# Expert 0's second weights: three raw units loaded in steps 26 to 30, and all four splits ahead of the last four first-layer blocks

## The chip, the cores and the metric

One core of one Trainium2 chip runs the kernel; the other cores are idle. The metric is the device time of one launch, in microseconds (us), lower is better. TensorE (PE) does the matrix products, VectorE (DVE) and ScalarE (ACT) read what it left in PSUM and work elementwise, GpSimd (POOL) issues the indirect transfers, and SyncE (SP) issues the plain ones.

## What is computed

Attention over 8 batches of 8 heads (576 positions, 64 features), with a plain 32-wide causal window for half of the heads and a dilated one for the rest, and behind it a mixture of eight experts, where each of the 4608 rows goes to the one expert with the largest gate logit:

```python
logits = x @ w_gate
expert_idx = np.argmax(logits, axis=1)
...
for e in range(E):
    mask = expert_idx == e
    ...
    h = np.maximum(xe @ w1[e], 0.0)      # 512 -> 1024
    ye = h @ w2[e]                       # 1024 -> 512
    out[mask] = gate_w[mask, None] * ye
```

## The kernel before

**Attention** runs as a software pipeline of 36 tiles of 128 positions. `step(n)` holds one stage of each of several tiles: scores of tile n, the transposes and the exponential of n-1, the product with v of n-2, the transposes of the rows for the gate of n-3, logits of n-4. Queries and keys of a tile are loaded five steps ahead (`load_qk`, 576 KB), values three steps ahead (`load_v`, 520 KB), both by SP. Every nine tiles `route` ranks the rows by expert; that of the last nine tiles runs as a tail behind the last step: DVE makes a one-hot tile `s1` and a block tile `b1` for each of nine tiles (L552, L560), PE sums them into `tb` (L571), and seven DVE operations over 128x320 tables (L647, L651 and five recorded under L441) give the row lists `both_i` that the later gathers read.

**Expert 0** starts early, on 256 rows taken from the first half of the sequence. Its weights are eight *units* of 128x1024: units 0 to 3 are the first layer, 4 to 7 the second. A unit is loaded by SP into one of three buffers `raw` (L829) and then *split* into a rounded high part (ACT, L730, two casts of 128x512) and the rest (DVE, L731, two subtractions); a product of the split numbers takes three matrix products. The first layer makes eight blocks of h; block f is twelve products into a PSUM tile `hps` (L846), a relu on ACT (L857) and a subtraction on DVE (L858), after which `hps` is free. Blocks 0 to 3 are made in the attention's last steps. Blocks 4 to 7 come behind `att.close()`, with two PSUM buffers for blocks 4, 6 and 7 (tag A) and one for block 5 (tag D): block 7 needs the buffer of block 4.

`att.close()` gives back the memory of the attention's pools, among them `fix` (qkr, vr, the constants `ca` that L552 reads) and `ap`. The pools opened behind it lie in that memory: `ph` with the h tiles first, then `pw1` with units 4 to 7.

**The second layer** of expert 0 follows in a section ordered by hand: `layer2(0, range(6))`, `layer2(1, range(6))` (18 products each, L877; block f of h with unit 4 + f/2), then the gathered rows of the next blocks are turned (`r0.prep_x`, L913), and the rest of expert 0 and the experts 1 to 7 follow.

**What sets the order.** Inside `manual_schedule` the named engines keep the order of the program. Steps 0 to 34 are such a section, for PE, DVE, ACT and SP; expert 0's second layer is another, for PE, DVE and ACT. What lies outside (step 35 on, the route's tail, blocks 4 to 7 and the splits of units 4 to 7) is put in order when the program is built: each engine's queue is filled with whatever is ready by the builder's own estimate, and among ready instructions the one that stands first in the program goes first. On the chip each queue then runs in that fixed order. Loads of `early_load` for units 4 to 6 stand in steps 36 to 38, outside the first section. `split_unit` is L726 to L734.

Of the kernel before, what the change touches and what calls it, by code (L numbers as in the profile page):

```python
# [159 lines left out]
def attention_moe_kernel(ctx, tc, qk, v, wg, w, cst, tok, end, slots, mask, zero, out):  # L160
# [48 lines left out]
    total = NPR * NT  # L209
# [470 lines left out]
    def all_gates():  # L680

        whole = [scr, none, late_g]
        for tab, to in zip(gtabs, whole):
            nc.scalar.dma_start(to, tab[:].rearrange("(p b) o -> p (b o)", p=P))
        whole = [g.bitcast(I32) for g in whole]
        nc.gpsimd.tensor_tensor(whole[0], whole[0], whole[1], op=ALU.add)
        nc.gpsimd.tensor_tensor(whole[0], whole[0], base.bitcast(I32), op=ALU.add)
        nc.gpsimd.tensor_tensor(both_i[:, :NBK, 1], whole[2], whole[0], op=ALU.add)
        nc.sync.dma_start(list_d[:].rearrange("(p b) o -> p b o", p=P), both_i)
# [33 lines left out]
    def new_unit(grp):  # L723
        return pools["w", grp].tile([P, 2, DF], F32R, tag=f"w{grp}", name="wu")

    def split_unit(grp, raw):  # L726
        u = new_unit(grp)
        for i in range(2):
            sl = slice(i * DM, (i + 1) * DM)
            nc.scalar.copy(u[:, 0, sl], raw[:, sl])  # L730
            nc.vector.tensor_tensor(  # L731
                u[:, 1, sl], raw[:, sl], u[:, 0, sl].bitcast(F32), op=ALU.subtract
            )
        return u  # L734
# [346 lines left out]
    def at(n, f, *a):  # L1081
        todo.setdefault(n, []).append(lambda: f(*a))
# [34 lines left out]
        at(FIRST_W + u, early_load, u)  # L1117
        at(FIRST_W + 2 + u, early_split, u)
    for u in range(4, 7):
        at(total + u - 4, early_load, u)  # L1120

    def early_layer1(f):
        n = first.ns
# [313 lines left out]
    for i in range(NE):  # L1437
        st_ = statics[i]
        nx = statics[i + 1] if i + 1 < NE else None
        if i == 0:  # L1440
            for f in range(4, 8):
                st_.layer1([f])
                raw = early.pop(f) if f in early else st_.load(f)
                st_.units.append(split_unit(1, raw))
            r0, r1 = rest0
            with tc.manual_schedule(engines=ENGS):
                ahead = nx.ahead

                def bring(u):
                    ahead[u] = nx.load(u)  # L1450

                def part(u):
                    nx.units.append(split_unit(c if u < 4 else a, ahead.pop(u)))
                    if u < 5:
                        bring(u + 3)

                def some_gates(n):
                    for _ in range(n):
                        gates_later.pop(0)()

                nx.begin()
                r0.fetch_x()
                nx.fetch(0)
                r1.fetch_x()
                nx.fetch(1)
                for u in range(3):
                    bring(u)
                st_.layer2(0, range(6))
                some_gates(1)
                st_.layer2(1, range(6))  # L1470
                r0.prep_x()
                nx.fetch(2)
                some_gates(1)
                st_.layer2(0, range(6, 8))
                r0.layer1([0])
                some_gates(1)
                nx.prep(0)
                nx.fetch(3)
                part(0)
                some_gates(1)  # L1480
                r0.layer1([1])
                some_gates(1)
                r0.turn([0])
                r1.prep_x()
                r0.turn([1])
                st_.layer2(1, range(6, 8))
                some_gates(1)
                r0.layer2(range(4))
                part(1)
                nx.prep(1)  # L1490
                some_gates(1)
                r1.layer1([0])
                some_gates(1)
                nx.prep(2)
                part(2)
                some_gates(1)
                r1.layer1([1])
                r1.turn([0])
                nx.prep(3)
                r1.turn([1])  # L1500
                part(3)
                r0.layer2(range(4, 8))
                part(4)
                r1.layer2()
                all_gates()
                r0.close()
                r1.close()
            loaded += [(nx, a, u, ahead.pop(u)) for u in range(5, 8)]
            a, b_, c = c, a, b_
            continue  # L1510
        with tc.manual_schedule(engines=ENGS):
            one_place(i)
        a, b_, c = c, a, b_
# [51 lines left out]
```

## Time and profile before

| what | us |
|---|---|
| median of three runs | 627.34 |
| lowest and highest | 626.08, 628.61 |
| the profiled execution, its own time | 627.71 |
| its span in the profile | 625.9 |

The profiled execution has 1.81 us around its span. In a row of the timeline the columns are start, duration, engine, line, operation, output<-inputs, form and count; a bracket gives the time for which the engine stood idle just before it, and who ended that. SPq is SP's queue: the row is the issue of a transfer, not the transfer.

### The profile page before, as it was taken

What the parts mean: (1) busy time and instruction counts of PE and PEld (TensorE: products, weight loads), DVE (VectorE), ACT (ScalarE), POOL (GpSimd) and SP (SyncE); (2) the same over time, 40 slices, a digit from 0 to 9 for tenths busy, and PEclk for the clock granted to TensorE, in tenths of its full rate; (3) what the DMA queues carried; (4) which work ended last, traced back from release to release, by engine and by line L of the source; (5) the groups of instructions that cost most, each with busy time, mean ns of one, the idle gap of its engine ahead of it and who ended that gap; (6) DMA issues with size and microseconds to landing.
All of it is one profiled execution on the core that took longest, in us unless ns stands there. A gap on an engine that the chain in (4) does not pass through costs nothing. (4 is left out here: it accounts for less than half of the span.)

```text
span 625.9 us, 13313 instructions
## 1 busy us (share of the span) xinstructions
PE 601.3 (96%) x5299; PEld 490.4 (78%) x5299; DVE 340.5 (54%) x754; ACT 313.2 (50%) x606; POOL 249.3 (40%) x296
## 2 busy tenths in 40 slices
PE   7999999999989999999999999999999999999992
PEld 6877787788878888788888888888888888888771
DVE  3876787888593544563457255625643573453000
ACT  2668766676533541563456256535644563552110
POOL 0336666476826620451245125312522341253520
PEclk8999999999999999999999999999999999999997
DMA  8999999994237650573476267717743763476710
GB/s 319 411 384 414 413 403 410 396 331 139 66 99 230 208 185 29 181 257 117 151 241 231 84 221 240 241 55 236 259 162 112 243 234 119 172 241 252 276 49 21
DMA packets 43359, 138.17 MB, mean 221 GB/s; under 512 B 9008, under 2 KB 10416, under 8 KB 43248
## 3 DMA queue, kind: packets, MB, share of 16 engines
q1 hardware_dynamic: 23088, 78.30, 34.5%
q0 software_dynamic: 19776, 58.52, 27.0%
q8 instruction: 42, 0.69, 0.4%
q10 hardware_dynamic: 432, 0.49, 0.2%
q14 instruction: 21, 0.17, 0.1%
HBM read 117.65 MB, written 21.63 MB: 223 GB/s over the span
## 5 line engine op out<-in xcount | busy, mean ns | idle before, releaser
L731 DVE TENSOR_TENSOR wu<-raw,wu 128x512 fp32r<-128x512 f32 x200 | 128.7, 687 | 103.7 <-ACT wu L730 103.7
L877 PE MATMUL yps<-wu,h 128*128 128x512 f32 x696 | 170.5, 396 | 0.4 <-DVE wu L731 0.4
L846 PE MATMUL hps<-x,wu 128*128 128x512 f32 (+1 forms) x720 | 164.0, 385 | 0.2 <-DVE h L858 0.2
L846 PEld LDWEIGHTS hps<-x,wu 128*128 128x128 f32 x720 | 132.0, 188 | 27.6 <-DVE h L858 0.7
L877 PEld LDWEIGHTS yps<-wu,h 128*128 128x128 f32 x696 | 128.0, 188 | 27.4 <-DVE wu L731 0.8
L730 ACT CAST wu<-raw 128x512 fp32r<-128x512 f32 x200 | 113.3, 621 | 27.8 <-DMA raw<-in_w_dram,wi 17.2
L922 POOL DMA_INDIRECT raw<-in_w_dram,wi x40 | 39.4, 985 | 98.3 <-DVE wu L731 90.7
L858 DVE SCALAR_TENSOR_TENSOR h<-hps,h 128x512 fp32r<-128x512 f32 (+1 forms) x60 | 40.1, 670 | 47.8 <-ACT h L857 47.6
L327 ACT COPY pts<-pt 96x512 f32<-96x512 f32 x72 | 41.9, 582 | 46.7 <-PE pt L322 45.9
L767 POOL DMA_INDIRECT out_dram<-y,both_i x30 | 32.7, 1091 | 80.2 <-ACT y L766 60.1
L857 ACT ACTIVATE h<-hps 128x512 fp32r<-128x512 f32 (+1 forms) x60 | 34.8, 581 | 59.4 <-PE hps L846 52.3
L766 ACT ACTIVATE y<-yps,both_i 128x512 f32<-128x512 f32 x28 | 19.3, 688 | 68.5 <-PE yps L877 36.1
L301 DVE TENSOR_REDUCE nm<-s 128x4 f32<-128x384 f32 x72 | 39.5, 550 | 25.0 <-PE s L290 24.5
L322 PE MATMUL pt<-ident,p 128*96 128x128 f32 x288 | 47.3, 288 | 3.2 <-ACT pts L327 2.8
L337 PE MATMUL o<-vr,pts 96*64 96x65 f32 x1152 | 43.7, 227 | 2.0 <-issue 1.9
L337 PEld LDWEIGHTS o<-vr,pts 96*64 96x64 f32 x1152 | 38.1, 139 | 9.4 <-issue 8.4
L369 POOL DMA_DIRECT2D x_d<-xs x36 | 20.6, 572 | 60.9 <-DVE xs L357 26.3
L756 POOL DMA_INDIRECT xg<-x_d,both_i x30 | 32.2, 1074 | 29.5 <-PE tpx L806 11.5
L306 DVE TENSOR_TENSOR d<-s,nm 128x384 f32<-128x384 f32 x72 | 40.1, 557 | 4.6
L316 ACT ACTIVATE p<-d 128x384 f32<-128x384 f32 x72 | 37.6, 524 | 6.6 <-DVE d L306 6.6
L973 PE MATMUL ypd<-wu,hd 128*128 128x512 f32 x168 | 40.4, 391 | 0.0
L941 PE MATMUL hpd<-wu,xd 128*128 128x512 f32 x168 | 40.2, 393 | 0.0
(169 smaller groups left out, 680.7 us busy)
## 6 DMA issues: line engine op xcount, KB each, us to landing
raw<-in_w_dram SPq DMA_DIRECT2D x64, 512.0 KB, 4.3
qkr<-in_qk_dram SPq DMA_DIRECT2D x36, 576.0 KB, 8.3
vr<-in_v_dram SPq DMA_DIRECT2D x36, 520.0 KB, 8.8
x_d<-xs POOLq DMA_DIRECT2D x44, 128.0 KB
t_in<-tab SPq DMA_DIRECT2D x3, 320.0 KB
x_d<-xs POOLq DMA_DIRECT2D x8, 112.0 KB
x_d<-xs POOLq DMA_DIRECT2D x8, 96.0 KB
tab<-in_zero_dram SPq DMA_DIRECT2D x2, 320.0 KB
```

The lines of the kernel that those rows point to most:

```text
L301: nc.vector.tensor_reduce(st["nm", n][:, g], st["s", n][g], axis=AX.X, op=ALU.max)
L306: nc.vector.tensor_tensor(st["d", n][:, g], st["s", n][g], st["nm", n][:, g].broadcast_to([P, HP, KB]), op=ALU.subtract,)
L322: nc.tensor.transpose(pt[:KB, h], st["p", n][:, g, h], ident)
L327: nc.scalar.copy(st["pts", n][:, g], st.pop(("pt", n))[:KB])
L337: nc.tensor.matmul(st["o", n][QB * j : QB * (j + 1), g, h], lhsT=pts[:, g, h, QB * j : QB * (j + 1)], rhs=vr[:KB, n % NRV, a : a + DH + 1] ...
L730: nc.scalar.copy(u[:, 0, sl], raw[:, sl])
L731: nc.vector.tensor_tensor(u[:, 1, sl], raw[:, sl], u[:, 0, sl].bitcast(F32), op=ALU.subtract)
L846: nc.tensor.matmul(hps[:, : self.ns], lhsT=u[:, wpart, fs], rhs=self.x[:, xpart, c, : self.ns], start=(k == 0), stop=(k == 11),)
L858: nc.vector.scalar_tensor_tensor(h[:, 1, :n], hps[:, :n], 0.0, h[:, 0, :n].bitcast(F32), op0=ALU.max, op1=ALU.subtract,)
L877: nc.tensor.matmul(yps, lhsT=self.h[f][:, hpart, ts], rhs=u[:, wpart, fs], start=f == 0 and k == 0, stop=f == 7 and k == 2,)
L941: nc.tensor.matmul(hps, lhsT=self.x[:, xpart, c], rhs=u[:, wpart, ns], start=(k == 0), stop=(k == 11),)
L973: nc.tensor.matmul(self.yps, lhsT=self.h[f // 4][:, hpart, f % 4], rhs=u[:, wpart, fs], start=f == 0 and k == 0, stop=f == 7 and k == 2,)
```

## The change

Units 4, 5 and 6 are loaded in steps 26, 28 and 30, inside the hand-ordered section, in place of steps 36, 37 and 38. Behind `att.close()` the loop that made block f and split unit f in turn becomes two loops: first the four splits (with the load of unit 7 in the last), then the four blocks.

```diff
     for u in range(4, 7):
-        at(total + u - 4, early_load, u)
+        at(total + 2 * u - 18, early_load, u)
...
         if i == 0:
             for f in range(4, 8):
-                st_.layer1([f])
                 raw = early.pop(f) if f in early else st_.load(f)
                 st_.units.append(split_unit(1, raw))
+            for f in range(4, 8):
+                st_.layer1([f])
             r0, r1 = rest0
```

`total` is 36. Step 26 also holds `clear_rows`, five plain transfers of SP that stand ahead of the load of unit 4.

## Rows read from the trace of the kernel before

**Rows 1.** The page: busy time, share of the span and instructions of each engine.

```profile
PE 601.3 (96%) x5299; PEld 490.4 (78%) x5299; DVE 340.5 (54%) x754; ACT 313.2 (50%) x606; POOL 249.3 (40%) x296
```

**Rows 2.** Busy time by stretch: start and end, length, busy time of each engine (instructions), granted TensorE clock, busy share of the DMA engines, GB/s.

```profile
100.00:110.00 10.00, 10.00 (x217) 8.52 (x209) 8.43 (x22) 6.75 (x14) 6.84 (x11) 1.00 1.03 410
...
181.00:194.00 13.00, 11.66 (x55) 8.87 (x56) 8.70 (x19) 5.00 (x12) 5.43 (x5) 1.00 0.60 189
194.00:223.00 29.00, 29.00 (x147) 24.19 (x146) 13.27 (x28) 14.93 (x28) 19.80 (x20) 1.00 0.66 213
...
300.00:460.00 160.00, 160.00 (x741) 131.69 (x740) 84.69 (x134) 84.86 (x154) 57.55 (x55) 1.00 0.60 199
```

**Rows 3.** Waits of PE between 181 and 194 us: who waited for whom, us in total, times, longest.

```profile
PE yps L877 <- DVE wu L731: 1.2, 3, 0.4
PE hps L846 <- DVE h L858: 0.2, 1, 0.2
```

**Rows 4.** Timeline of SP's queue: the loads of expert 0's second weights, and two loads of queries, that behind `clear_rows` and the last one.

```profile
89.92 0.38 SPq L829 DMA_DIRECT2D raw<-in_w_dram  x1
...
97.94 0.90 SPq L829 DMA_DIRECT2D raw<-in_w_dram  x2
...
118.23 0.54 SPq L213 DMA_DIRECT2D qkr<-in_qk_dram  x1
...
129.91 0.33 SPq L213 DMA_DIRECT2D qkr<-in_qk_dram  x1
...
183.11 6.94 SPq L829 DMA_DIRECT2D raw<-in_w_dram  x4
```

**Rows 5.** Timeline of ACT from 180 us on: relu of blocks 4 and 7, casts of units 4, 6 and 7.

```profile
180.25 0.38 ACT L857 ACTIVATE h<-hps 128x256 fp32r<-128x256 f32 x1 [7.04 <-DVE s L552]
180.56 1.14 ACT L730 CAST wu<-raw 128x512 fp32r<-128x512 f32 x2
...
183.18 1.14 ACT L730 CAST wu<-raw 128x512 fp32r<-128x512 f32 x2
184.21 0.39 ACT L857 ACTIVATE h<-hps 128x256 fp32r<-128x256 f32 x1
186.57 1.14 ACT L730 CAST wu<-raw 128x512 fp32r<-128x512 f32 x2 [1.97 <-DMA raw<-in_w_dram]
```

**Rows 6.** Timeline of PE: blocks 4 to 6, the route's sums between them, block 7, the second layer.

```profile
173.88 2.41 PE L846 MATMUL hps<-x,wu 128*128 128x256 f32 x18
...
178.47 0.31 PE L571 MATMUL tb<-b,s 128*128 128x320 f32 x1
178.62 0.51 PE L846 MATMUL hps<-x,wu 128*128 128x256 f32 x3
...
179.96 0.96 PE L571 MATMUL tb<-b,s 128*128 128x320 f32 x2
181.14 1.70 PE L846 MATMUL hps<-x,wu 128*128 128x256 f32 x12 [0.22 <-DVE h L858]
182.68 1.80 PE L877 MATMUL yps<-wu,x 128*128 128x512 f32 x7
...
188.88 2.96 PE L877 MATMUL yps<-wu,x 128*128 128x512 f32 x12
191.68 1.55 PE L877 MATMUL yps<-wu,h 128*128 128x512 f32 x6
193.07 0.60 PE L913 MATMUL tpx<-ident,xg 128*128 128x128 f32 x4
```

**Rows 7.** Timeline of DVE (and one row of POOL): the tail of the route, the splits and the blocks.

```profile
175.14 0.15 DVE L531 SCALAR_TENSOR_TENSOR last_i<-last_i,last_f 128x1 int32<-128x1 int32 x1
175.21 0.17 DVE L637 CAST plc<-plc_i 128x9 f32<-128x9 int32 x1
...
179.83 0.33 DVE L552 TENSOR_SCALAR s<-ca,plc,pay 128x128 fp32r<-128x128 f32 x1
...
180.66 0.42 DVE L858 SCALAR_TENSOR_TENSOR h<-hps,h 128x256 fp32r<-128x256 f32 x1 [0.20 <-ACT h L857]
181.00 0.48 DVE L647 TENSOR_SCALAR scr<-tb 128x320 f32<-128x320 f32 x1
181.40 0.68 DVE L731 TENSOR_TENSOR wu<-raw,wu 128x512 fp32r<-128x512 f32 x1
182.00 0.48 DVE L651 TENSOR_TENSOR scr<-tb,scr 128x320 f32<-128x320 f32 x1
...
183.40 0.41 DVE L858 SCALAR_TENSOR_TENSOR h<-hps,h 128x256 fp32r<-128x256 f32 x1
183.74 0.48 DVE L441 CUSTOM_DVE_ANT_0 base<-t_in,none 128x640 uint16<-128x640 uint16 x1
...
185.49 2.02 POOL L756 DMA_INDIRECT xg<-x_d,both_i  x1 [8.90 <-DVE both_i L441]
```

**Rows 8.** The granted TensorE clock at the start of the kernel, by stretch (columns as in rows 2), and PE's timeline there.

```profile
10.00:10.50 0.50, 0.50 (x20) 0.38 (x12) 0.07 (x1) 0.00 (x0) 0.00 (x0) 0.97 1.03 420
10.50:11.00 0.50, 0.50 (x4) 0.35 (x2) 0.49 (x1) 0.00 (x0) 0.00 (x0) 0.50 1.00 403
...
17.00:17.50 0.50, 0.50 (x14) 0.46 (x12) 0.14 (x1) 0.00 (x0) 0.00 (x0) 0.70 1.04 420
...
8.31 0.35 PE L274 MATMUL s<-mk 64*64 64x384 bf16 x2 [1.27 <-DVE d L306]
...
11.97 1.09 PE L322 MATMUL pt<-ident,p 128*96 128x128 f32 x4 [0.67 <-ACT pts L327]
...
17.53 0.64 PE L322 MATMUL pt<-ident,p 128*96 128x128 f32 x4
```

## The prediction, made before the changed kernel was run

> **What bounds the kernel now.** I read the page first: PE is busy for 601.3 us, 96% of the span, and no other engine passes 54% [rows 1]. The stretches say whether that share is even: from 194 to 223 us PE fills 29.00 of 29.00 us, from 300 to 460 us 160.00 of 160.00 [rows 2]. So a microsecond that PE gains or loses ahead of 194 us should reach the end nearly whole. The place of the change is thinner: 11.66 of 13.00 us from 181 to 194 us [rows 2], and the waits there name the split's subtraction L731 (1.2 us) and L858, which frees a PSUM buffer (0.2 us) [rows 3]. The timeline gives the whole size of the hole. The route's last sum ends at 179.96 + 0.96 = 180.92 us and the turn of the next rows starts at 193.07 us: 12.15 us [rows 6]. In it lie block 7, 1.54 us from its start to the next row's, and 36 products of the second layer at 0.233 us each (twelve from 188.88 to 191.68 us), 8.40 us [rows 6]. The remaining 2.2 us are holes, and they are the most that any order of this place can win.
>
> **The moved loads.** By the program units 4 to 6 are loaded in steps 36 to 38. The trace tells otherwise: one load leaves SP at 89.92 us and two at 97.94 us, some 80 us before the first cast at 180.56 us [rows 4, 5]; the next load of weights, at 183.11 us, is unit 7's [rows 4]. The builder had already lifted them, since they stood outside the hand-ordered section and their buffers were free. Inside it they will keep their place, behind `clear_rows` and in the two steps after the next ones, from about 117 us (`clear_rows` is followed by a load of queries at 118.23 us [rows 4]) to a little after 129.91 us, where the last load of queries, step 30's, leaves SP [rows 4]. So the edit makes these loads some 30 us later, not earlier, and they still land nearly 50 us ahead of their use: nothing for expert 0. What they are now moved past is SP's loads of queries and values and POOL's stores of rows, in a stretch where the DMA engines are as full as where the loads lie today (1.03 of their time at 100 to 110 us, with PE at 10.00 of 10.00 [rows 2]). Unit 4 may hold back the load of queries at 118.23 us by one issue, 0.4 us or so (the row at 89.92 us lasts 0.38 [rows 4]), and by up to one landing; that load is five steps ahead of its use. I take 0. Bounds: 0, and at most the three loads' own transfer, 3 x 0.52 MB at 410 GB/s [rows 2], 3.9 us.
>
> The Trainium skill (Trainium Kernel Development and Optimization, Key Constraints) says that transfers issued from SP, ACT and POOL all run on the same 16 DMA engines and interleave. By it the 1.57 MB are paid by whatever else is queued, up to the 3.9 us above; the trace agrees that the engines are full, but PE shows no loss where the loads lie now, so the sum by the row is 0.
>
> **The splits' earliest start.** Could they now run in ACT's empty stretch before 180 us? ACT stood idle for 7.04 us before the relu of block 4, although that block's twelve products were done by about 176 us (18 products in 2.41 us from 173.88 [rows 6]), and what ended the wait is L552, done at 179.83 + 0.33 = 180.16 us [rows 5, 7]. The h tile does not use L552's output; it lies in the memory of the closed pool `fix`, whose constants L552 is the last to read. Units 4 to 7 lie in memory of `fix` and `ap`, so the same release holds them. I take 180.16 us as the earliest start of both splits and relus, before and after.
>
> **The new order behind that release.** Before, ACT took relu 4, casts 4, relu 5, casts 5 and so on [rows 5]. After, the casts stand first in the program and three units are in memory: six casts from 180.25 us at 0.57 us each (two in 1.14 [rows 5]), done at 183.7 us, and only then the relus, 0.38 us each. DVE is the tighter engine. From row to row a table operation takes 0.40 us (181.00 to 181.40), a split's subtraction 0.60 (181.40 to 182.00), a block's L858 0.34 (183.40 to 183.74) [rows 7]. DVE always has both kinds waiting; the seven table operations stand earlier in the program and take turns with the subtractions, since each hangs on the one before. From 181.0 us, 7 x 0.40 + 6 x 0.60 = 6.4 us, so it is 187.4 us before the three units are through. Now L858 of block 4, which ran at 180.66 us [rows 7], can go. Or unit 7 goes first: its buffer is freed by unit 4's second subtraction as today, at about 183.1 us, its load takes 3.46 us to the cast (183.11 to 186.57 [rows 4, 5]), and its subtractions stand ahead of L858 in the program: 2 x 0.60 more. L858 of block 4 thus ends at 187.8 or at 189.0 us, 7 to 8 us later than today.
>
> **What waits for it.** On PE block 7 needs block 4's buffer, as it does now [rows 6]. But PE need not stand empty: the queue is filled with what is ready, and the hand-ordered section holds nothing back. Its first DVE instruction, L531 of the first gate, already runs at 175.14 us ahead of the route's L637 [rows 7], and PE already slips blocks between the route's sums [rows 6]. So the products of h blocks 0 to 3, which exist, go first: 12 of the first 18, as their units come, until about 185.9 us. Then both block 7 and h block 4 are missing. After L858: 1.54 us for block 7 and 24 products of 0.233 us, 5.6 us, so 7.1 us. The turn of rows starts at 187.85 + 7.1 = 195.0 us, or at 189.05 + 7.1 = 196.2 us, against 193.07 us: **+1.9 or +3.1 us**. The 2.2 us of holes are not won but replaced by a longer one. The turn's gather is issued at 185.49 us behind `both_i` [rows 7]; without a block between the table operations that stays within 0.5 us, so the gather is not late. Nothing else is freed: PE is full behind it [rows 2]. I take the later figure, because program order puts unit 7 first and its cast can be there by then: 627.71 + 3.1 = 630.8 us on the profiled execution, which lies 0.37 us above the median, so about 630.6 us for the median to be measured.
>
> **The clock.** PE would be empty from about 185.9 to 187.8 or 189.0 us, after five us of piecemeal work. At the start of the kernel, after a stretch of such holes (1.27 us idle before 8.31 us), the granted clock goes from 0.97 of the 2.4 GHz level to 0.50, the 1.2 GHz level, near 10.5 us and comes back within 17.0 to 17.5 us [rows 8]. Four transposes take 1.09 us there against 0.64 after [rows 8]: 41% of the work is lost while it lasts. It lasts 6.8 us there. If it happens here, with half to all of such a stretch filled by dense work, it costs 3.4 to 6.8 us x 0.41, 1.4 to 2.8 us. In the 13 us from 181 us the clock was 1.00 with the present holes [rows 2].
>
> The Trainium skill (TensorE: Matmul & The Clock Gate, Part 1: The HAM clock gate) says that half rate is the default state and activity releases it. By it a long enough hole costs the extra 1.4 to 2.8 us; the fall at 10.5 us agrees, and no row of before has so long a hole at this place.
>
> **Rivals.**
> - *Splits first, with the clock falling*: 627.3 + 1.9 to 3.1 + 1.4 to 2.8, 630.6 to 633.2 us. For it: the new hole, 1.9 to 3.1 us, is longer than the 1.27 us of rows 8. Against: it is a single one. 25%.
> - *PE's queue keeps block 7 ahead of the second layer*: PE is empty from 180.92 us to L858; then 1.54 + 8.40 us, the turn at 197.8 to 199.0 us, +4.7 to +5.9, with the clock up to +8.7: 632.0 to 636.0 us. Against it stands L531 at 175.14 us. 11%.
> - *Not slower: the splits are not held by L552*, because their memory is free once the values are used. Then they run in ACT's 7 us, the blocks find their relus first, and PE wins up to 2.2 us: 625.1 to 626.5 us. It decides if a cast L730 starts before 180 us. Against it: the idle 7.04 us [rows 5]. 6%.
> - *The change does not do what it says*: loads early already, and the builder orders the queues so that the relus still come between. 627.3 us, +-0.9. 13%.
> - *The loads slow the attention*: +1.3 to +3.9 us, from one load's transfer to all three, decided by scores late after step 28. 4%.
>
> **How the numbers follow.** The forecast (splits first, no fall of the clock) has 41% and 629.2 to 630.6 us. A measurement of this kernel can tell 0.5%, 3.1 us, from no change: 630.5 us upward is slower. That is about a quarter of the forecast's 41 (10), all 25 and 11 of the first two rivals, and 1 of the last: 47%. Faster needs 624.2 us, more than the holes hold: 3%. The same: 50%. For 8 in 10, I leave out the lower part of the gain and the upper part of the block-7 case: 626.2 to 635.0 us.
>
> **What would show it.** Right: loads of weights between 115 and 133 us; six casts in a row on ACT from about 180.25 us, and the relu of block 4 behind them; L858 of block 4 after 187 us; PE idle near 186 to 189 us on L858; the turn L913 at 195 to 196.2 us, that much later than 193.07; equal times from step to step before 180 us. Wrong: casts before 180 us; L858 of block 4 between the subtractions near 184 us; block 7 ahead of the second layer; a granted clock of 0.5 near 190 us; or a shift at 195 us that is gone by 300 us, which would mean that PE does not carry it to the end.

## The result, and the profile of the changed kernel

The changed kernel takes 631.04 us (median, 630.27 to 632.27), the kernel before 627.39 us in the same comparison (626.08 to 628.61): ratio 1.0064, 95% interval 1.0045 to 1.0083. It is slower, by 3.65 us in the medians. The profiled execution took 631.1 us with a span of 629.3 us (before: 627.71 and 625.9).

PE's work is what it was, against 601.3 us in [rows 1]; this is the first line of the page:

```profile
PE 601.9 (96%) x5299; PEld 489.9 (78%) x5299; DVE 340.4 (54%) x754; ACT 313.4 (50%) x606; POOL 250.8 (40%) x296
```

SP's queue, to be held against [rows 4]. The three loads have moved from 90 to 98 us to 118 to 131 us:

```profile
118.15 0.64 SPq L829 DMA_DIRECT2D raw<-in_w_dram  x1
118.88 0.40 SPq L213 DMA_DIRECT2D qkr<-in_qk_dram  x1
...
124.69 1.33 SPq L829 DMA_DIRECT2D raw<-in_w_dram  x1
...
131.41 0.38 SPq L829 DMA_DIRECT2D raw<-in_w_dram  x1
```

ACT's timeline from 179 to 188 us, against [rows 5]. Six casts now stand in a row, behind the same idle stretch and the same releaser, and the relus of blocks 4 to 6 come after them:

```profile
179.90 3.22 ACT L730 CAST wu<-raw 128x512 fp32r<-128x512 f32 x6 [7.08 <-DVE s L552]
183.02 0.92 ACT L857 ACTIVATE h<-hps 128x256 fp32r<-128x256 f32 x3
186.41 1.14 ACT L730 CAST wu<-raw 128x512 fp32r<-128x512 f32 x2 [2.47 <-DMA raw<-in_w_dram]
```

DVE's timeline, against [rows 7]. Table operations and subtractions take turns to 186.6 us; the last subtraction of unit 6 and both of unit 7 follow, and only at 188.44 us, where it was 180.66 us, the first L858:

```profile
181.21 0.69 DVE L731 TENSOR_TENSOR wu<-raw,wu 128x512 fp32r<-128x512 f32 x1 [0.17 <-ACT wu L730]
181.82 0.48 DVE L651 TENSOR_TENSOR scr<-tb,scr 128x320 f32<-128x320 f32 x1
...
186.64 1.89 DVE L731 TENSOR_TENSOR wu<-raw,wu 128x512 fp32r<-128x512 f32 x3
188.44 1.07 DVE L858 SCALAR_TENSOR_TENSOR h<-hps,h 128x256 fp32r<-128x256 f32 x3
```

PE's timeline, against [rows 6]. Fourteen products of the second layer go ahead of block 7; then PE stands for 2.05 us until L858 has given it block 4's buffer:

```profile
179.54 0.97 PE L571 MATMUL tb<-b,s 128*128 128x320 f32 x2
180.57 0.50 PE L877 MATMUL yps<-wu,x 128*128 128x512 f32 x1
181.96 3.73 PE L877 MATMUL yps<-wu,x 128*128 128x512 f32 x11 [0.88 <-DVE wu L731]
185.53 0.40 PE L877 MATMUL yps<-wu,h 128*128 128x512 f32 x1
186.37 0.49 PE L877 MATMUL yps<-wu,h 128*128 128x512 f32 x1 [0.45 <-DVE wu L731]
188.91 1.69 PE L846 MATMUL hps<-x,wu 128*128 128x256 f32 x12 [2.05 <-DVE h L858]
190.44 1.09 PE L877 MATMUL yps<-wu,h 128*128 128x512 f32 x4
191.37 2.96 PE L877 MATMUL yps<-wu,x 128*128 128x512 f32 x12
194.17 1.54 PE L877 MATMUL yps<-wu,h 128*128 128x512 f32 x6
195.55 0.60 PE L913 MATMUL tpx<-ident,xg 128*128 128x128 f32 x4
```

PE's waits between 180 and 197 us, against [rows 3]: L731 ends as much waiting as before (1.3 for 1.2 us), L858 2.0 us where it was 0.2.

```profile
PE hps L846 <- DVE h L858: 2.0, 1, 2.0
PE yps L877 <- DVE wu L731: 1.3, 2, 0.9
```

Stretches (columns as in [rows 2]): the microseconds of the hole, and the full stretches behind it. PE's clock stays at 1.00 through the hole, and PE is full again at once, so it has nothing to catch up with:

```profile
187.00:188.00 1.00, 0.00 (x0) 0.00 (x0) 1.00 (x3) 0.55 (x2) 1.00 (x1) 1.00 0.63 250
188.00:189.00 1.00, 0.09 (x1) 0.09 (x1) 1.00 (x3) 0.00 (x0) 1.00 (x1) 1.00 0.56 147
...
197.50:226.50 29.00, 29.00 (x147) 24.20 (x146) 13.29 (x28) 14.78 (x27) 18.83 (x19) 1.00 0.59 195
300.00:460.00 160.00, 160.00 (x740) 131.66 (x740) 83.67 (x133) 84.50 (x154) 57.06 (x54) 1.00 0.58 196
```

**Where the time went.** The route's last sum ends at 179.54 + 0.97 = 180.51 us, the turn starts at 195.55 us: 15.03 us (the rows are rounded) against 12.15 in [rows 6], 2.9 us more. This *distance* is the measure used below. DVE sets it: 8.40 us pass from the last sum to the start of block 7, which waits for L858, and 6.63 us of PE's work follow. The end of the attention differs from trace to trace (the maxima of its last scores start between 154.2 and 156.6 us, the two runs on a slower chip left out), and here it came 0.4 us earlier than before, so the turn itself is 2.48 us later. From there every `y` of expert 0 to expert 7 (L766) up to 560 us is 2.45 to 2.47 us later: the loss is carried whole. In the last 64 us the difference grows to 3.44 us. I don't count that 0.99 us to the change, since kernels of either order have it or not: the stretch from the `y` near 550 us to the last one takes 63.90 us before and 64.89 after, but 63.90 and 64.68 in two other kernels with the order of before, 63.81 and 64.30 in two executions with the order of after. In these two traces it arises between 562 and 574 us, where DVE's L994, which waits for the gather `own`, starts 0.54 us later than the 2.45 make it, and two casts that wait for a load of weights 0.98 us later. The medians differ by 3.65 us, about 0.8 more than the 2.88 of the distance; no trace of the other five executions shows where that arose (see the step on the clock below).

### The profile page after: what moved, and what is told of

Same layout as the page of the kernel before. It is cut to its first block, busy times and chain, and to the rows that moved or that the text cites. A ratio compares the mean times of both kernels' runs of the same rounds, so it can differ in the third digit from the quotient of the medians.

```text
span 629.3 us, 13313 instructions
## 1 busy us (share of the span) xinstructions
PE 601.9 (96%) x5299; PEld 489.9 (78%) x5299; DVE 340.4 (54%) x754; ACT 313.4 (50%) x606; POOL 250.8 (40%) x296
## 5 line engine op out<-in xcount | busy, mean ns | idle before, releaser
L731 DVE TENSOR_TENSOR wu<-raw,wu 128x512 fp32r<-128x512 f32 x200 | 129.3, 689 | 106.2 <-ACT wu L730 106.1
L858 DVE SCALAR_TENSOR_TENSOR h<-hps,h 128x512 fp32r<-128x512 f32 (+1 forms) x60 | 39.8, 668 | 47.4 <-ACT h L857 47.1
L301 DVE TENSOR_REDUCE nm<-s 128x4 f32<-128x384 f32 x72 | 39.5, 549 | 26.6 <-PE s L290 26.6
L766 ACT ACTIVATE y<-yps,both_i 128x512 f32<-128x512 f32 x28 | 19.3, 688 | 68.5 <-PE yps L877 36.1
L756 POOL DMA_INDIRECT xg<-x_d,both_i x30 | 33.5, 1116 | 30.8 <-PE tpx L806 11.5
L306 DVE TENSOR_TENSOR d<-s,nm 128x384 f32<-128x384 f32 x72 | 40.0, 557 | 4.6
L316 ACT ACTIVATE p<-d 128x384 f32<-128x384 f32 x72 | 37.6, 525 | 6.5 <-DVE d L306 6.5
## 6 DMA issues: line engine op xcount, KB each, us to landing
vr<-in_v_dram SPq DMA_DIRECT2D x36, 520.0 KB, 10.2
```

What stands on the lines that cost most here:

```text
L306: nc.vector.tensor_tensor(st["d", n][:, g], st["s", n][g], st["nm", n][:, g].broadcast_to([P, HP, KB]), op=ALU.subtract,)
L731: nc.vector.tensor_tensor(u[:, 1, sl], raw[:, sl], u[:, 0, sl].bitcast(F32), op=ALU.subtract)
L858: nc.vector.scalar_tensor_tensor(h[:, 1, :n], hps[:, :n], 0.0, h[:, 0, :n].bitcast(F32), op0=ALU.max, op1=ALU.subtract,)
```

## Experiments

Two theories stood against each other. Mine: the order alone costs the time, through two queues in a row (DVE's subtractions ahead of L858, and L858 ahead of block 7 on PE), and the moved loads cost nothing. The rivals: the loads slow the attention or the weights; or one place alone, such as block 4's PSUM buffer, makes the whole loss; and, for a better version, that another engine or an earlier start could win the holes.

| kernel | distance, us | ratio to before, 95% interval |
|---|---|---|
| before | 12.15 | 1 |
| after | 15.03 | 1.0064 [1.0045, 1.0083] |
| e1_loads | 12.13 | 1.0001 [0.9986, 1.0016] |
| e2_order | 15.04 | 1.0070 [1.0055, 1.0085] |
| e2_order_again | 15.05 | 1.0044 [1.0021, 1.0067] |
| e3_unit7_last | 13.83 | 1.0030 [1.0018, 1.0041] |
| e4_block4_first | 13.78 | 1.0028 [1.0015, 1.0042] |
| e5_pool_half | 13.12 | 1.0023 [1.0010, 1.0036] |
| e6_consts_out | 6.60 | 1.0133 [1.0116, 1.0150] |
| e8_consts_rows_out | 6.45 | 1.0029 [1.0016, 1.0041] |
| e10_unit7_by_hand | 7.88 | 1.0043 [1.0027, 1.0060] |
| e11_splits_first | 13.22 | 1.0009 [0.9987, 1.0031] |

In e6, e8 and e10 the route itself ends later, so there the distance alone says nothing; the text gives the turn.

### The two halves of the change: e1_loads and e2_order

The loads of the changed kernel in the loop of before:

```diff
-        at(total + u - 4, early_load, u)
+        at(total + 2 * u - 18, early_load, u)
```

> The loads alone: units 4, 5 and 6 are loaded in steps 26, 28 and 30; blocks and splits in turn, as before the change. Theory (the order of the splits makes the whole loss, the loads nothing): the time of the kernel before, ratio 1.000 +-0.002; from the end of the route's last sum on PE (L571) to the first turn of rows (L913) 12.15 us, as before; the steps up to 180 us as long as before, +-0.5 us. Rival (the loads in the full stretch slow the attention): +1.3 to +3.9 us, the route's last sum that much later than 180.9 us.

The order of the changed kernel with the loads of before:

```diff
             for f in range(4, 8):
-                st_.layer1([f])
                 raw = early.pop(f) if f in early else st_.load(f)
                 st_.units.append(split_unit(1, raw))
+            for f in range(4, 8):
+                st_.layer1([f])
```

> The order alone: all four splits ahead of blocks 4 to 7, the loads where they were in the program (lifted to 90 to 98 us by the builder). Theory: the whole loss, ratio 1.004 to 1.0065; from the route's last sum to the turn of rows 15.0 us, with one wait of PE on L858 of about 2 us in it. Rival (part of the loss comes from the loads, for instance the 1 us that appears behind 560 us): 1.002 to 1.004, and no extra microsecond behind 560 us.

Measured: e1_loads 627.17 us against 627.19, with the distance of before to 0.02 us; its loads leave SP at 117.32, 124.02 and 130.67 us, and its one line of waits from 181 to 194 us is that of before:

```profile
PE yps L877 <- DVE wu L731: 1.2, 3, 0.4
```

e2_order has the distance of after to 0.01 us and 631.24 us against 627.19. So the loads cost nothing that can be told (at most 0.16% by the interval), and the order is the whole loss at this place. But 4.05 us in the medians is more than the 2.9 us of the distance, and I timed the kernel once more:

> The kernel before with only the order of the changed kernel (all splits in the program ahead of blocks 4 to 7), once more. Its first timing gave 1.0070, about 1 us more than the 2.9 us by which the turn is later. If that excess was the run-to-run variation of the gathers in expert 7, the ratio is 1.0040 to 1.0055 now; if it belongs to the order, 1.0060 to 1.0075. The distance from the route's last sum to the turn is 15.0 us either way.

Measured: 1.0044 [1.0021, 1.0067], distance 15.05 us. 2.9 us are 1.0046, which lies in the interval of the repetition and of the changed kernel, and below that of the first timing. The excess did not come back, which fits executions that differ in expert 7. That this was it in the first timing is not shown, and there is a second candidate: the profiled execution, the fastest of the six (629.69 us), has a mean granted clock of 0.989, the other five 0.982 to 0.986, so that PE spent more time at the 1.2 GHz level in them. (The repetition and e11 ran on a chip on which the kernel before takes 638.12 us; the ratios are to that.)

### Which of the waits: e3_unit7_last and e4_block4_first

Unit 7 split behind the blocks, the rest as in the changed kernel:

```diff
-            for f in range(4, 8):
-                raw = early.pop(f) if f in early else st_.load(f)
-                st_.units.append(split_unit(1, raw))
+            for f in range(4, 7):
+                st_.units.append(split_unit(1, early.pop(f)))
             for f in range(4, 8):
                 st_.layer1([f])
+            st_.units.append(split_unit(1, st_.load(7)))
```

> The changed kernel, but unit 7 is loaded and split behind the four blocks; units 4, 5 and 6 are still split ahead of them. Theory (DVE's queue sets when block 4 is done, each subtraction ahead of it costs 0.6 us): L858 of block 4 starts 1.2 us earlier than in the changed kernel, PE's wait on L858 falls from 2.05 to 0.85 us, and the distance from the route's last sum to the turn of rows from 15.0 to 13.8 us; time 1.2 us below the changed kernel, ratio to before 1.003 to 1.004. Rival (ACT's casts or the load of unit 7 set it): no change of that distance.

Measured: 13.83 us, 629.06 us. DVE's timeline shows L858 at 187.25 us, 1.19 earlier than in the changed kernel, with unit 7's subtractions now behind it:

```profile
187.25 1.08 DVE L858 SCALAR_TENSOR_TENSOR h<-hps,h 128x256 fp32r<-128x256 f32 x3
188.25 1.28 DVE L731 TENSOR_TENSOR wu<-raw,wu 128x512 fp32r<-128x512 f32 x2
```

The distance falls by the same 1.2 us: two subtractions at 0.60 us are 1.2 of the 2.9 us, and where the prediction chose between +1.9 and +3.1 us, this is the switch.

In this execution the clock fell in the middle of the place. The stretch from 182 to 185 us here and in the changed kernel (columns as in [rows 2]):

```profile
182.00:185.00 3.00, 3.00 (x7) 2.43 (x8) 3.00 (x7) 1.96 (x6) 0.00 (x0) 0.50 0.30 74
```

```profile
182.00:185.00 3.00, 2.89 (x10) 1.45 (x10) 3.00 (x7) 1.94 (x6) 0.00 (x0) 1.00 0.31 93
```

In the 3 us ahead of it PE had done the same in both, 1.89 and 1.90 us of work. The fall cost nothing here: a product took 0.43 us instead of 0.23, but the 14 products, which wait for DVE anyway, end at 186.88 us in this trace and at 186.86 in the changed kernel's.

Block 4 alone ahead of the splits:

```diff
             if i == 0:
+            st_.layer1([4])
             for f in range(4, 8):
                 raw = early.pop(f) if f in early else st_.load(f)
                 st_.units.append(split_unit(1, raw))
-            for f in range(4, 8):
+            for f in range(5, 8):
                 st_.layer1([f])
```

> The changed kernel, but block 4 stands ahead of the four splits; blocks 5 to 7 stay behind them. Theory (every block that waits behind the splits holds PE, the missing PSUM buffer only the first of them): block 7 runs at 181 us as before the change, but the second layer still wants h block 5, whose L858 comes behind eight subtractions at about 189 us; 21 products of 0.233 us follow; from the route's last sum to the turn of rows 13.6 us, 1.4 us less than changed and 1.4 us more than before; ratio 1.002 to 1.004. Rival (the buffer of block 4 is the whole cause): 12.2 us and the time of before.

Measured: 13.78 us, 629.15 us. Block 7 gets its buffer nearly at once (0.2 us, as in [rows 3]), and PE waits one step later, first for the second part of an h block, then for the gather; its waits from 180 to 197 us:

```profile
PE yps L877 <- DVE h L858: 1.0, 1, 1.0
PE tpx L913 <- DMA xg<-x_d,both_i: 0.9, 1, 0.9
PE yps L877 <- DVE wu L731: 0.4, 1, 0.4
PE hps L846 <- DVE h L858: 0.2, 1, 0.2
```

So block 4's buffer is only the first thing that is late. With it on time 1.6 us of the loss remain.

### Less work for DVE: e5_pool_half

Before's order, with the second half of each of three units subtracted by GpSimd:

```diff
-    def split_unit(grp, raw):
+    def split_unit(grp, raw, second=None):
...
-            nc.vector.tensor_tensor(
+            (second if i and second else nc.vector).tensor_tensor(
...
-                st_.units.append(split_unit(1, raw))
+                st_.units.append(split_unit(1, raw, nc.gpsimd if f < 7 else None))
```

> The kernel before (blocks and splits in turn, loads as before), but the second of the two subtractions of units 4, 5 and 6 runs on GpSimd, which is idle from 176.6 to 185.5 us. Theory (DVE is the engine that holds the second layer at this place; each subtraction taken from it is worth up to 0.6 us): three subtractions less on DVE, the halves come every 0.6 to 1.3 us from two engines, and PE finds each of them in time: from the route's last sum to the turn of rows 10.0 to 10.6 us against 12.15, ratio to before 0.9965 to 0.998. Rival (1.27 us for a subtraction on GpSimd is too slow, or the two engines slow each other): 11.5 us or more, no gain.

A miss: the distance is 13.12 us, 0.97 more than before, where I expected 1.5 to 2.1 less; 628.26 us against 626.88. DVE's timeline, from the row before GpSimd starts:

```profile
179.53 0.68 DVE L731 TENSOR_TENSOR wu<-raw,wu 128x512 fp32r<-128x512 f32 x1
180.13 0.48 DVE L651 TENSOR_TENSOR scr<-tb,scr 128x320 f32<-128x320 f32 x1
180.53 0.41 DVE L858 SCALAR_TENSOR_TENSOR h<-hps,h 128x256 fp32r<-128x256 f32 x1
180.87 0.86 DVE L441 TENSOR_TENSOR none<-t_in,scr 128x320 int32<-128x320 int32 x1
181.65 1.78 DVE L731 TENSOR_TENSOR wu<-raw,wu 128x512 fp32r<-128x512 f32 x1
183.35 1.59 DVE L441 CUSTOM_DVE_ANT_0 base<-t_in,none 128x640 uint16<-128x640 uint16 x1
```

and GpSimd's:

```profile
179.92 4.68 POOL L731 TENSOR_TENSOR wu<-raw,wu 128x512 fp32r<-128x512 f32 x3 [5.18 <-ACT wu L730]
```

While GpSimd subtracts, DVE's operations with both inputs in SBUF stretch: 0.68 to 1.78 us, 0.48 to 1.59 and to 0.86. L858 and L651, which read one input from PSUM, keep their 0.41 and 0.48 us. DVE gives up 1.10 + 1.11 + 0.38 = 2.6 us and is spared three subtractions, 1.8 us, so the work taken from it costs it more than it weighed. PE's waits for L731 grow from 1.2 to 2.5 us. GpSimd's own subtraction takes 1.56 us, where those that it makes in the attention of the kernel before (L745) take 1.26 to 1.29; beside them DVE's operations with an input in PSUM keep their length (L306 0.56 us, L357 0.69).

The Trainium skill (SBUF — State Buffer, SBUF: two separate sides) says that a DVE operation with two SBUF inputs and a GpSimd operation that reads SBUF take one pair of ports in turns, each for its whole instruction. The rows agree, the two operations with a PSUM input above all.

### An earlier start: e6_consts_out, e8_consts_rows_out, e10_unit7_by_hand

The prediction only argued that casts and relus are held by the memory of the closed pools. Here the constants move to a pool that stays open to the end of the route; everything else is the changed kernel:

```diff
-    rows_i = fix.tile([P, NPR - 1, NT], I32, name="rows_i")
-    rows_f = fix.tile([P, NT], F32, name="rows_f")
-    ca = fix.tile([P, C_ATT - C_TRI], F32, name="ca")
+    rows_i = late.tile([P, NPR - 1, NT], I32, name="rows_i")
+    rows_f = late.tile([P, NT], F32, name="rows_f")
+    ca = late.tile([P, C_ATT - C_TRI], F32, name="ca")
```

> The changed kernel, but the constants ca and the row numbers rows_i, rows_f lie in the last pool of the attention instead of in fix, so that the memory of units 4 to 7 and of h is free when the values and the last rows xs are. Theory (the release by L552 holds splits and relus until 180 us): the casts no longer start behind L552 but when the last store of rows (x_d<-xs) has landed, near 174.5 us; the queues of ACT and DVE stand behind the first cast, so the route's last sum comes 3 to 5 us later than 180.5; from there to the turn of rows 6 to 7.5 us instead of 15.0, the turn at 190.5 to 192.5 us, ratio to before 0.995 to 0.999. Rival (DVE's load alone sets it and an earlier release wins nothing): the turn stays at 195 us and the ratio at 1.005 to 1.007.

Measured: the casts no longer wait for L552. ACT's timeline:

```profile
173.46 1.14 ACT L730 CAST wu<-raw 128x512 fp32r<-128x512 f32 x2 [5.81 <-DMA t_in<-tab]
```

So the step is shown: the release of `fix` held them. But the turn comes at 196.22 us and the kernel takes 634.86 us (the profiled execution, the fastest of four, 632.13). The builder had put the first subtraction on DVE ahead of the route's L490, for a start that did not come; DVE stands 7.77 us behind it, and PE with it:

```profile
PE tl L485 <- DVE lt L490: 6.1, 1, 6.1
```

PE's clock falls in this hole, at 172 us, and is at 0.50 until 178.8 us, which adds to the loss by an amount that I did not separate.

The next edit takes that wait away too, by moving the tiles of rows that the last stores read:

```diff
-            xs = ap.tile([P, 2, 4, DH], F32, name="xs", bufs=3)
+            xs = late.tile([P, 2, 4, DH], F32, name="xs", bufs=3)
```

> As the kernel with the constants moved out, and the rows xs too, so that no store stands between the end of attention's reads and the splits. Theory: casts start at 169 to 170 us, most subtractions fall into DVE's idle time up to 174 us, the second layer's first twelve products run between the route's sums; the casts of unit 7 wait for its load until about 175.5 us and hold the blocks' relus and DVE's part of the route behind them by 1 to 2 us; the route's last sum at 181 to 183 us, the turn of rows 6 to 7.5 us behind it, at 188 to 190 us, ratio to before 0.992 to 0.995. Rival (as above, DVE's total sets it): the turn not before 192 us.

Measured: casts at 169.72 us, 10.2 us earlier than in the changed kernel (ACT's timeline):

```profile
169.72 1.14 ACT L730 CAST wu<-raw 128x512 fp32r<-128x512 f32 x2
...
178.35 1.14 ACT L730 CAST wu<-raw 128x512 fp32r<-128x512 f32 x2 [3.91 <-DMA raw<-in_w_dram]
```

and still 628.27 us against 626.88, slower. The subtractions now stand between the route's steps on DVE, so the route's last sum ends at 187.23 us, 31.0 us after the start of the last scores' maxima (L301), against 24.4 before. The places, and the gather behind them, are later with it (gather issued at 190.20 us, 185.49 in [rows 7]); PE's waits between 160 and 197 us end with it:

```profile
PE hps L846 <- DVE h L858: 1.5, 1, 1.5
PE hps L846 <- DVE x L858: 1.4, 1, 1.4
PE tpx L913 <- DMA xg<-x_d,both_i: 0.9, 1, 0.9
```

Unit 7 had to wait for its load inside this stretch (the 3.91 us on ACT; DVE 2.02 us behind it), so a third kernel loads it behind the blocks and splits it in the section ordered by hand:

```diff
-                raw = early.pop(f) if f in early else st_.load(f)
-                st_.units.append(split_unit(1, raw))
+                st_.units.append(split_unit(1, early.pop(f)))
...
+            raw7 = st_.load(7)
...
                 st_.layer2(0, range(6))
                 some_gates(1)
+                st_.units.append(split_unit(1, raw7))
```

> As the kernel with constants and rows moved out, but unit 7 is loaded behind the blocks and split in the hand-ordered section behind the first 18 products of the second layer. Theory: nothing on DVE waits for that load inside the route; the route's last sum at 180.5 to 181.5 us, but unit 7's two subtractions now stand between the table operations and make the row lists, and so the gathered rows, 1.2 us later; the turn of rows at 188 to 190 us, within 1 us of the kernel without this edit. If the load of unit 7 was a cost in that kernel, this one is 1 us or more faster; if not, it is the same or slower.

Measured: 629.47 us, not better than e8 (the intervals overlap). The profiled execution is the slowest of six, 632.22 us; in it the turn is at 196.73 us, the last sum at 188.86. Its subtractions are out of the way, but its first cast stands on ACT ahead of a relu and waits 4.93 us for the load, and the L858 of that relu stands on DVE ahead of the route's L610. Two of DVE's waits from 160 to 197 us, and PE's longest:

```profile
DVE h L858 <- ACT h L857: 3.3, 1, 3.3
...
DVE scr L647 <- PE tb L571: 2.3, 1, 2.3
```

```profile
PE tb L571 <- DVE s L552: 3.3, 1, 3.3
```

The 2.3 us are the clock's: it falls 2.0 us into the hole in which PE stands and is at 0.50 from 180.6 to 187.4 us. PE's work from 181.86 us to the last sum takes 7.0 us there and would take about 4.4 at the full clock (an estimate from the lengths of the same products at 1.00 in [rows 6]). That part needn't be there in every execution: the two with a mean granted clock of 0.988 and 0.989 took 627.82 and 629.41 us.

In all three the earlier start is real and is spent on the route.

### DVE's order turned round: e11_splits_first

Before's order, with subtractions and blocks ahead of the table:

```diff
-                st_.layer1([f])
+                st_.layer1([f], ahead=True)
                 raw = early.pop(f) if f in early else st_.load(f)
-                st_.units.append(split_unit(1, raw))
+                with tc.high_priority():
+                    st_.units.append(split_unit(1, raw))
...
-                nc.scalar.activation(h[:, 0, :n], hps[:, :n], AF.Relu)
+                with tc.high_priority() if ahead else contextlib.nullcontext():
+                    nc.scalar.activation(h[:, 0, :n], hps[:, :n], AF.Relu)
```

(L858 stands in the same block.)

> The kernel before, with one thing changed: in the stretch after the route's last sums VectorE takes the subtractions of units 4 to 6 and the blocks' second parts ahead of the table's reductions (the five operations from `scr` to the last `base` that give the places). No operation is added or left out. My theory says that PE's holes of 1.4 us behind L731 and L858 in that stretch come from VectorE's order alone, and that the table has some 4 us to spare (its gather is issued at 185.49 us, takes about 3.5 us, and the turn reads it at 193.07). Then the turn comes 1.0 to 1.4 us earlier from the route's last sum (distance 10.7 to 11.1 us instead of 12.15), and the ratio is 0.9975 to 0.999. The rival, which the runs that freed the splits early support: VectorE's total sets the end whatever comes first. The two subtractions and two second parts now ahead of the table (some 2.8 us) make the gather late by as much, the turn waits for the gather, and the distance is 12 to 13 us, the ratio 1.000 to 1.001.

Measured: the rival's side, and a little beyond its 12 to 13 us, 13.22 us; 638.77 us against 638.12, a ratio that can't be told from 1. PE's timeline (line numbers are one or two higher in this kernel: L731 is the cast, L732 the subtraction, L915 the turn):

```profile
193.91 0.50 PE L879 MATMUL yps<-wu,x 128*128 128x512 f32 x1 [1.09 <-ACT wu L731]
195.41 2.13 PE L879 MATMUL yps<-wu,x 128*128 128x512 f32 x8 [0.99 <-DVE wu L732]
...
203.42 0.63 PE L915 MATMUL tpx<-ident,xg 128*128 128x128 f32 x4 [0.32 <-DMA xg<-x_d,both_i]
```

The gather is issued at 197.67 us, 7.5 us after the last sum at 190.20 (before: 4.6), as the rival had it. But PE's holes did not shrink either: the longest hole is now a wait for a cast on ACT, where the relus that I put ahead stand between the casts. That they made it late is likely and not shown. So this run doesn't show that no order is better than before's; it shows that this one isn't.

## The prediction, step by step

- **PE sets the end and a loss ahead of 194 us reaches it whole**: right. 2.48 us at the turn, 2.45 us at every `y` to 560 us.
- **The loads are moved later, and cost nothing**: right. Predicted from about 117 to a little after 129.91 us, measured 118.15 to 131.41; alone they give 1.0001 (e1_loads). Unit 4 held back the load of queries by one issue, as its row shows. The bound of 3.9 us (3.8 by its own figures) is ruled out.
- **Casts and relus are held until L552's end**: right, and the cause, which was only argued, is shown by e6 and e8. The rival that they might run in ACT's idle 7 us would not have been a gain in this order: given that start, e8 is slower.
- **Six casts first, then DVE's alternation, L858 of block 4 at 187.8 or 189.0 us**: right. Table operations and subtractions alternate, unit 7 goes first, and L858 starts at 188.44 us. Counted from the route's last sum that is 7.9 us; the prediction had 7.7 to its start (189.0, less 0.34, less 180.92). DVE's wait of 0.17 us for the first cast, which the sum has not, is most of the 0.2. e3 confirms the choice between the two.
- **PE takes products of the second layer, then waits**: right, with one term mis-sized. I counted 12 products ahead of the hole; there are 14. The products of h block 4 with its first part need the relu alone, and the relus were done by 183.94 us. So 22 products stand behind L858, not 24, which is 0.47 us less; block 7 starts 0.27 us later after the last sum than the sum had it (8.40 us for 8.13). The two leave 0.2: the distance is 15.03 us instead of 12.15 + 3.1 = 15.25, its change +2.9 where the sum had +3.1.
- **The clock does not fall**: right for the profiled execution, 1.00 through the hole of 2.05 us, and open for the others. The mean granted clock of the six executions is 0.988 in the profiled one and one more, 0.985 in two and 0.983 in two. The 0.988 goes with 15.1 us at the 1.2 GHz level, near the start and behind the last product; 0.985 and 0.983 would be some 4 and 6 us more of it (an estimate: each microsecond at 0.50 takes half of its share of the 629 us off the mean; e3's profiled execution has 0.985 and 18.8 us). Of 29 executions of the kernel before (those beside e1 to e4) 27 have 0.987 or more. So four of the six executions of the changed kernel had more time at the lower level than the profiled one, and no trace shows where; e3 shows a fall at this very place, where it cost nothing. Whether it is the 0.8 us in the medians that the distance leaves is open: the two executions at 0.988 took 631.10 and 630.54 us, the other four 630.27 to 632.27. The Trainium skill (TensorE: Matmul & The Clock Gate, Part 1: The HAM clock gate) has half rate as the default state that activity releases; e3's trace agrees that it can come back here (0.50 from 182.0 to 185.4 us), the changed kernel's does not show it.
- **Block 7 does not stand ahead of the second layer**: right; 14 products stand before it.
- **630.6 us**: measured 631.04. The figure itself has a slip: 630.8 less 0.37 is 630.4. And 631.04 lies above the 629.2 to 630.6 us that the forecast gave itself, inside the range of the rival with the falling clock; that the forecast's mechanism held is known from the trace, not from the time. The profiled execution's +3.4 us is 2.45 us from this place and 0.99 from expert 7, rounded. The prediction's +3.1 contains nothing for expert 7 and 0.6 us more at the turn than came (0.2 of the term above, 0.4 of an attention that ended earlier), so the two partly cancel, and that the time came so near is in part luck: the mechanism, not the last half microsecond, is what was confirmed.

## What to carry to other kernels

Of work that waits for one release, look for the part that frees a buffer or feeds the next stage, and ask where it stands in the queue of the tightest engine. Here bulk preparation as a block ahead of small consumers cost 2.9 us on top of 12 against the two in turn (e2); putting the consumers ahead of everything won nothing either (e11). When a stall is put down to one engine's order, add up that engine's work over the stretch first: starting part of it earlier or putting it elsewhere moves the stall (to the route, to the gather), unless that other place has time to spare. Moving three loads by some 30 us cost nothing here, since they still landed long before their use (e1), so look at where a load is issued in the trace before paying for moving it in the program.

## What the runs showed of the hardware

**GpSimd elementwise work beside DVE** stretched DVE's operations with two SBUF inputs by up to 1.11 us each, 2.6 us over three GpSimd subtractions of 1.56 us, and left those with a PSUM input alone (e5). I had planned that run with the two engines as independent, and named their slowing each other only as a rival.

**The clock fell in some executions, ahead of the change or at its place.** In the same stretch, with the same work ahead of it, PE was granted 0.50 in e3 and 1.00 in the changed kernel (above). It also fell in e6 at 172 us, after 3 us in which PE stood, and in e10 at 180.6 us, after it had stood for 2. On another chip it fell in the attention: in e2_order_again the time from the last scores' maxima to the route's last sum is 31.0 us, where it is 24.3 to 24.4 us in before and after. Its stretches there:

```profile
162.00:166.00 4.00, 1.97 (x36) 1.55 (x36) 0.00 (x0) 2.56 (x6) 3.08 (x4) 0.99 0.03 3
166.00:170.00 4.00, 3.42 (x17) 1.62 (x16) 1.56 (x4) 1.17 (x2) 3.39 (x6) 0.50 0.21 66
170.00:174.00 4.00, 4.00 (x48) 3.48 (x45) 0.98 (x3) 1.81 (x5) 3.10 (x5) 0.66 0.59 133
```

PE was busy for 1.97 of 4.00 us, and then ran at 0.50, the 1.2 GHz level, until about 173 us. The profile names no full cause of the idle time: PE's largest waits there are 1.2 us for an exponential (L316) and 1.1 us with no releaser ("issue"). e11_splits_first, on the same chip, shows the same fall (0.53 from 166 to 170 us). What starts it on that chip is open. The distance behind it, 15.05 us, is that of e2_order on the first chip (15.04), which is why it and not the span carries the argument.
